# Retimed plan, squares of v as a step, half of the rest on POOL, weights two places on: attention, Fourier mixing and a feed-forward block on one core

## Chip, cores and metric

The kernel runs on one core of a Trainium2 chip. The metric is device time in microseconds (us), the median of several runs. Five engines of the core matter: PE (TensorE, matmuls; PEld is its weight load), DVE (VectorE), ACT (ScalarE), POOL (GpSimd) and SP (SyncE, which issues most DMAs). Each works through its own queue in order, and they wait for each other by semaphores. PSUM, where PE writes, has eight banks here: one for the value products, three called `ps`, two called `h` and two called `acc`.

## What is computed

Block-causal attention over 8 batches x 8 heads, 576 positions of 64 dimensions; then, for each batch, a two-dimensional Fourier transform whose real part is added to x, a normalization, and a feed-forward block 512 to 2048 to 512.

```python
scores = scale * np.matmul(q, k.transpose(0, 1, 3, 2))
scores = np.where(block_i >= block_j, scores, -1000000000.0)   # blocks of 64 positions
attn = np.exp(scores - np.max(scores, axis=-1, keepdims=True))
attn = attn / (np.sum(attn, axis=-1, keepdims=True) + 1e-09)
x = np.matmul(attn, v)                  # heads side by side: 8 x 576 x 512
u = x + np.real(np.fft.fft(np.fft.fft(x, axis=1), axis=2))
un = (u - np.mean(u, -1)) / np.sqrt(np.var(u, -1) + 1e-06)
out = u + np.maximum(un @ w_ch1, 0.0) @ w_ch2
```

## The kernel before

Numbers are carried as pairs: a high part that PE multiplies, and the rest that is left of it.

**Heads.** For each head, `load_head` brings q and k (`raw`), `lead` makes the rounded high part on ACT (L275), `lead_copies` sends two copies of it by SP's DMAs into the `rest` tile, and `rest` makes the two halves of the remainder, each 64 x 576, on DVE (L285, L286). `max_part` (four parts, n = 0 to 3) multiplies and reduces the row maxima on DVE (L358, and L361 for the last block); `shift` transposes them on PE (L183) and sends them as an additional row into `lead`. `scores` (four pieces) multiplies, takes the exponential twice on ACT (L401 in 16 bits, L402 in 32), and POOL subtracts (L403), so that `ph` and `pl` are the two parts of the probabilities. `values` multiplies them by v; at its end DVE computes `DEN`, its reciprocal and x (L438 to L441), which SP writes to `xd` for two heads at a time.

**v.** Once for two heads, `load_v` loads V (one buffer) and `split_v` makes it into `VH` and `VL`: ACT squares and sums V into `vacc` (two buffers; L299; its unused product goes into the scratch `tmp`), a matmul with ones sums over partitions, DVE makes a power of two from it (L304 to L308), ACT scales (L310) and DVE takes the remainder (L311). `DEN` reads the scale out of the same `vacc`.

**Fourier and feed-forward.** After a batch's eight heads, `mirror` reads `xd` back by POOL's indirect DMAs; `folded` adds on DVE (L517, L518, scratch `tmp`) and splits on ACT and DVE into `fs` (L485, L486); `stage1`, `stage2_sin` and `stage2_cos` multiply. `norm` and `turn` normalize and transpose. Each group of two tiles then gives one feed, whose steps `first` (tile `h`, then `gh` on ACT and `gl` on DVE) and `second` (tile `acc`) PE works through.

**Weights.** They come as 64-bit numbers. `weight_loads` lands them in parts of the big tile `W` that are still free, or in `stage`; `weight_single` turns them into 32 bits with six DVE instructions for two (L786, L788, L790), and ACT squares them (L792); `weight_scale` makes the scale; `weight_parts` writes the high part on ACT (L814) and the remainder on DVE (L815). The 32 bits of weight i lie in place i + 1 of `W`, which part i + 1 overwrites.

**The plan.** The order of work is made at build time by a planner. Each lane (heads, preparation, v, maxima, scores, values, transform) yields steps; a `Step` has its time on PE (`cost`), a `chain` of what follows on other engines, written as an engine letter with a duration ("A0.25", Q for SP's queue, L for latency, G for POOL), the steps it comes `after` in time, the steps that must only have been issued (`need`), and a `place` that sets who goes first. The planner keeps a booked queue for each engine, adds `HOP` between engines, and takes, of the steps that are ready, the one with the lowest place; if none is ready, PE gets a step of the current feed, the filler. A step that is ready only in less than `MARGIN` (0.3) waits while there is filler. PE keeps exactly this order. A step with `bank` takes a PSUM bank; until the first feeds, the banks of `h` and `acc` are lent as well. The order on the other engines is set when the program is built, out of the order in which steps were issued. The weights are a side lane, issued while the queue of the first engine of a step is short.

Of the kernel before, what the change touches and what calls it, by code (L numbers as in the profile page):

```python
# [20 lines left out]
DM = H * D  # L21
FF = 4 * DM
P = 128
# [9 lines left out]

HOP = 0.2
MARGIN = 0.3
# [7 lines left out]
KM = D + 8  # L43
KS = KM + 1


# [76 lines left out]
class Step:  # L123
# [12 lines left out]
    def __post_init__(self):  # L136
        self.chain = [(x[0], float(x[1:])) for x in self.chain]

# [26 lines left out]
def tile_attn_fourier_ffn(  # L165
# [61 lines left out]

    W = const.tile([P, 2 * NF + 1, 2, DM], F16, name="W")
    inv_w = const.tile([P, 1], F32, name="inv_w")
# [51 lines left out]

    def rest(h):

        x0, x1, raw = REST[h % NB], LEAD[h % NB].bitcast(F32), raws.pop(h)
        nc.vector.tensor_tensor(x0[0:D, 0:S], raw[:, 0:S], x1[0:D, 64:64 + S], op=ALU.subtract)  # L285
        nc.vector.tensor_tensor(x0[D:P, S:], raw[:, S:], x1[0:D, 64 + S:], op=ALU.subtract)  # L286

# [4 lines left out]
    vraw = {}  # L292

    def split_v(g):

        V = vraw.pop(g)
        acc = work.tile([P, 4], F32, name="vacc", bufs=2)
        junk = work.tile([P, DM], F32, name="tmp", bufs=2).bitcast(F16)[:, 0:5 * 2 * D]
        nc.scalar.activation(junk, V.rearrange("p c h d -> p (c h d)"), AF.Square, accum_out=acc[:, 0:1])  # L299
        t = ps_tile()  # L300
# [13 lines left out]
    def head_lane():  # L314
        for h in range(B * H):
            yield Step(
                lambda: load_head(h), 0.0, ("Q0.6", "L2.5"), (("T2", h - 2),) if h > 1 else (), ("L", h), place=h - 2.2
            )

    def prepare_lane():  # L320
        for h in range(B * H):
            yield Step(
                lambda: lead(h), 0.0, ("A1.05",), (("L", h),), ("T", h), place=h - 1.0,
                need=(("S", h - NB, 2),) if h >= NB else (),
            )
# [12 lines left out]

    def max_part(h, n):
# [9 lines left out]
        for i, (j, lo, hi) in enumerate(parts):  # L349
# [4 lines left out]
            at += hi - lo  # L354
        at = 0
        for j, lo, hi in parts:
            to = 5 if lo else j
            nc.vector.tensor_reduce(m[:, to:to + 1], t[:, at:at + hi - lo], axis=AX.X, op=ALU.max)  # L358
            at += hi - lo
        if n == 3:  # L360
            nc.vector.tensor_tensor(m[:, 4:5], m[:, 4:5], m[:, 5:6], op=ALU.max)  # L361

    MAXPARTS = (((0, 0, 64), (1, 0, 192), (4, 512, 576)), ((2, 0, 320),), ((3, 0, 448),), ((4, 0, 512),))

# [86 lines left out]
    def score_lane():  # L451
        for h in range(B * H):
            for n, (i, at, chunks) in enumerate(PIECES):
                w = sum(x[2] for x in chunks)
                e = 0.085 + 0.00083 * w
                yield Step(
                    lambda n=n: scores(h, n), w / 1200.0, (f"A{2 * e}", f"G{0.19 + 0.002 * w}"),
                    (("X", h), ("TC", h), ("T2", h)), ("S", h, i) if n else None, True,
                    need=(("V", h - 1, 2 * i),) if h else (), place=h,
                )  # L460

    def max_lane():
        for h in range(B * H):
            for n in range(4):
                yield Step(
                    lambda n=n: max_part(h, n), 0.05 + sum(x[2] - x[1] for x in MAXPARTS[n]) / 2000.0, (f"D{(0.6, 0.45, 0.55, 0.7)[n]}",),
                    (("T", h),), ("M", h) if n == 3 else None, True, place=h - 0.6,
                )
            yield Step(lambda: shift(h), 0.12, ("A0.25", "Q0.6", "L2.2"), (("M", h),), ("X", h), True, place=h - 0.6)

    def value_lane():
        for h in range(B * H):
            for n, c in enumerate(CHUNKS):
                yield Step(
                    lambda n=n: values(h, n), 0.09 * (5 - c), ("D0.9",) if n == 4 else (),
                    (("S", h, (0, 1, 1, 2, 2)[n]), ("N", h // 2)) + ((("V", h - 1, 4),) if h else ()), ("V", h, n),
# [13 lines left out]
    def fourier_steps(b):  # L490
# [125 lines left out]
        for name, op, width in (("c", ALU.add, 257), ("s", ALU.subtract, 256)):  # L616
            for c in (2, 0, 1):
                yield Step(
                    lambda c=c: folded(op, width, name, c), 0.0, ("D0.8", "A0.3", "D0.3"), (D_("u"),),
                    D_("f" + name) if c == 1 else None, place=place,  # L620
                )
            for m in range(2):
                yield Step(
                    lambda m=m: stage1(name, m), 0.87, ("A0.35", "D0.4"), (D_("f" + name),),
                    D_("z" + name) if m == 1 else None, True, place=place,
                )
            if name == "c":
                yield Step(stage1_tail, 0.62, ("A0.3", "D0.4"), (D_("fc"),), D_("zt"), True, place=place)
        for c in (2, 0, 1):
            yield Step(lambda: stage2_sin(c), 0.67, ("A0.3",), (D_("zs"),), D_("b", c), True, place=place)  # L630
            yield Step(
                lambda: stage2_cos(c), 0.78, ("D0.7", "D1.3" if b == 0 else "G2.4"), (D_("zc"), D_("zt"), D_("b", c)), D_("u", c), True,
                need=(("F", feed_number(b - 1, 2)),) if c == 2 and b == 4 else (), place=place,
            )
# [11 lines left out]
    def normalized_steps(us, keys, stores, place):  # L646
# [46 lines left out]
    def feed_steps(me, uh, ul, us, stores):  # L693
# [32 lines left out]
        def first_steps(f):  # L726
            for part in range(NK):
                last = part == NK - 1
                after = (("t", me, 0), ("t", me, 1)) + ((("g", me, f - 2),) if f > 1 else ()) if part == 0 else ()
                if me == 1:  # L730
                    after += (("w", NK * (f // NK) + part),)
                yield Step(
                    lambda part=part: first(f, part), 0.327, ("A0.3", "D0.35") if last else (), after,
                    ("g", me, f) if last else None,
                )

        def second_steps(f):
            for n in range(2):
                yield Step(
                    lambda n=n: second(f, n), 0.648, (), (("g", me, f),) + ((("w", NF + f),) if me == 1 else ()),  # L740
                    ("F", me) if f == NF - 1 and n == 1 else None,
# [20 lines left out]

    LANDS = [(17, 19, 21, 23)[i % 4] for i in range(NF)]
    LANDS += [25, 27, 29, 31, -1, -2, -3, 25, 27, 29, 31, -1, -2, -3, -1, -2]

# [15 lines left out]
    def weight_single(i):  # L781
        if loads[0] < i + 2:
            weight_loads(i)
        two = [(raw(j).rearrange("p (n x) -> p x n", x=2), W[:, j + 1].rearrange("p x n -> p (x n)").bitcast(I32)) for j in (i, i + 1)]
        for r, t in two:
# [24 lines left out]
    def weight_parts(i):  # L810
        t = W[:, i + 1].rearrange("p x n -> p (x n)").bitcast(F32)
        w = i // NF
        sc = wst[:, 4 * w + 1:4 * w + 2]
        nc.scalar.activation(W[:, i, 0], t, AF.Copy, scale=sc)  # L814
        nc.vector.scalar_tensor_tensor(W[:, i, 1], t, sc, W[:, i, 0], op0=ALU.mult, op1=ALU.subtract)  # L815

    def weight_lane():
        yield Step(lambda: weight_loads(0), 0.0, ("Q5",), (("L", 0),), ("load",))
        def single(i):
            return Step(  # L820
                lambda: weight_single(i), 0.0, ("D0.6", "D0.6", "D0.9", "D0.9", "D0.85", "D0.85", "A0.82", "A0.82"), (("load",),),
                "w32" if i == 2 * NF - 2 else None,
            )

        def scale(w):
            return Step(lambda: weight_scale(w), 0.1, ("D1.2",), (), ("scale", w), True)
# [128 lines left out]
```

## Time and profile before

| what | value |
|---|---|
| median of 3 runs | 1396.62 us (1396.25 to 1399.97) |
| profiled execution | 1401.47 us, its span 1399.7 us |
| mean granted TensorE clock | 0.938 |
| instructions | 25596 |
| memory traffic | 58.46 MB read, 18.87 MB written |

The profile lists busy times by engine, the same in slices or windows of time, groups of instructions by line, and waits. Most matmuls stand at one helper's line, L180, and transpositions at L183, so they are told apart by their tiles: `ps<-vacc,ones` is the sum over partitions of `split_v`, `ps<-ident,M` the transposition of `shift`. A row of waits names the engine that waited, its line and tile, what released it, the total, how often and the longest. A group's row gives count, busy time and mean ns of one instruction, then idle time just before it and who ended it. A timeline row gives start and duration in us, then in brackets the idle time before and its releaser.

### The profile page before, as it was taken

Reading aid. Unit: us, or ns where it says so; the run is one execution under the profiler, and the core shown is the slowest. Engines: PE = TensorE matmul, PEld = TensorE weight load, DVE = VectorE, ACT = ScalarE, POOL = GpSimd, SP = SyncE. Lnnn points to the kernel's source line nnn. Section 1 sums busy time; section 2 is a strip of 40 time slices with the busy share of each in tenths; the row PEclk is TensorE's granted clock in tenths of the full one; section 3 lists DMA queues with packets and bytes.
Section 4 is the critical chain, followed back from the end, with each engine's and each line's share of the span. In section 5 each row is a group of like instructions: output and inputs, shape, how many; then the busy total and the mean of one; then the engine's idle time right before and its main releaser. Section 6 shows DMA issues by size and latency. Waiting matters only on the chain.

```text
span 1399.7 us, 25596 instructions
## 1 busy us (share of the span) xinstructions
PE 1203.7 (86%) x10068; PEld 895.2 (64%) x10068; DVE 748.2 (53%) x1770; ACT 568.0 (41%) x1293; POOL 383.5 (27%) x484
## 2 busy tenths in 40 slices
PE   2546478988897999889998999898989899999998
PEld 1445356766675677566675767676667676766665
DVE  5996776456645564555537555755464634322211
ACT  3555546444453445443444444444443342111111
POOL 1323122232423243324232522343232431300000
PEclk9965679999899999989999999999999999999999
DMA  9655212232223112421322122312222101000000
GB/s 289 192 174 177 62 29 77 70 95 57 59 63 108 49 43 69 111 57 28 93 73 73 32 67 73 107 32 68 62 92 57 42 10 58 5 16 16 16 16 15
DMA packets 56168, 99.11 MB, mean 71 GB/s; under 512 B 7933, under 2 KB 26829, under 8 KB 55920
## 3 DMA queue, kind: packets, MB, share of 16 engines
q1 hardware_dynamic: 53760, 89.94, 23.0%
q0 software_dynamic: 2288, 7.54, 1.7%
q8 instruction: 79, 1.29, 0.4%
q14 instruction: 41, 0.34, 0.1%
HBM read 58.46 MB, written 18.87 MB: 55 GB/s over the span
## 4 chain that ended last, share of the span: by engine, by line
PE 66%; DVE 16%; DMA 7%; issue 4%; POOL 3%; ACT 3%; SPq 0%; DVEq 0%; POOLq 0%; ACTq 0%
PE acc L180 24%; PE h L180 24%; PE ps L180 14%; PE av L180 3%; DVE rest L286 2%; DVE rest L285 2%; DVE M L358 2%; DMA U<-xd,rows 2%; PE ps L183 2%; DMA V<-in_v_dram 1%; DVE W L790 1%; DVE W L788 1%; DMA W<-in_moe_w_ch_dram 1%; ACT tmp L299 1%; DVE tmp L517 1%
## 5 line engine op out<-in xcount | busy, mean ns | idle before, releaser
L180 PE MATMUL h<-uh,W 128*128 128x256 f16 x2304 | 455.4, 278 | 0.0
L403 POOL TENSOR_TENSOR pl<-p,ph 128x288 f16<-128x288 f32 (+1 forms) x256 | 245.5, 969 | 572.0 <-ACT p L402 477.6
L180 PEld LDWEIGHTS <-W 128*128 128x128 f16 x3456 | 330.9, 100 | 88.6 <-issue 4.2
L180 PE MATMUL acc<-W,gh 128*128 128x512 f16 x1152 | 352.1, 388 | 0.6 <-ACT gh L711 0.6
L180 PE MATMUL h<-ul,W 128*128 128x256 f16 x1152 | 319.3, 277 | 0.7 <-DVE ul L674 0.7
L712 DVE SCALAR_TENSOR_TENSOR gl<-h,gh 128x256 f16<-128x256 f32 x288 | 121.6, 422 | 358.1 <-ACT gh L711 356.0
L711 ACT ACTIVATE gh<-h 128x256 f16<-128x256 f32 x288 | 110.8, 385 | 360.4 <-PE h L180 351.9
L180 PE MATMUL acc<-W,gl 128*128 128x512 f16 x576 | 222.4, 386 | 3.7 <-DVE gl L712 3.7
L180 PE MATMUL ps<-lead 72*128 72x64 f32 (+2 forms) x714 | 210.5, 353 | 7.0 <-DVE vacc L304 3.6
L358 DVE TENSOR_REDUCE M<-ps 128x1 f32<-128x192 f32 (+2 forms) x353 | 138.3, 427 | 96.4 <-PE ps L180 95.6
L401 ACT ACTIVATE ph<-ps 128x512 f16<-128x512 f32 (+1 forms) x238 | 122.0, 513 | 86.0 <-PE ps L180 83.4
L180 PEld LDWEIGHTS ps<-lead 72*128 72x128 f32 (+1 forms) x714 | 131.7, 204 | 21.1 <-DVE vacc L304 4.2
L180 PEld LDWEIGHTS <-gh 128*128 128x128 f16 x1152 | 102.7, 100 | 59.6 <-issue 3.9
L180 PE MATMUL av<-VH,ph 128*128 128x65 f16 x960 | 122.0, 205 | 18.4 <-DVE x L441 17.5
L180 PEld LDWEIGHTS <-ph 128*128 128x128 f16 x1920 | 107.6, 104 | 47.3 <-issue 23.4
L180 PE MATMUL av<-VH,pl 128*128 128x65 f16 x960 | 118.7, 202 | 19.8 <-POOL pl L403 19.7
L402 ACT ACTIVATE p<-ps 128x512 f32<-128x512 f32 (+1 forms) x238 | 122.4, 514 | 18.0 <-POOL pl L403 17.8
L180 PE MATMUL ps<-rest 128*128 128x192 f32 (+4 forms) x361 | 123.1, 349 | 0.5 <-ACT p L402 0.5
L180 PE MATMUL av<-VL,ph 128*128 128x64 f16 x960 | 120.3, 202 | 0.0
L180 PEld LDWEIGHTS <-pl 128*128 128x128 f16 x960 | 95.1, 103 | 23.7 <-POOL pl L403 23.4
L180 PEld LDWEIGHTS <-gl 128*128 128x128 f16 x576 | 57.3, 99 | 76.3 <-DVE gl L712 5.9
L180 PEld LDWEIGHTS ps<-rest 128*128 128x128 f32 x361 | 72.4, 201 | 10.5 <-ACT p L402 0.7
(171 smaller groups left out, 1310.3 us busy)
## 6 DMA issues: line engine op xcount, KB each, us to landing
raw<-in_qk_dram SPq DMA_DIRECT2D x64, 288.0 KB
rest<-lead SPq DMA_DIRECT2D x128, 144.0 KB
W<-in_moe_w_ch_dram SPq DMA_DIRECT2D x24, 512.0 KB
V<-in_v_dram SPq DMA_DIRECT2D x32, 320.0 KB
xd<-x SPq DMA_DIRECT2D x32, 256.0 KB
out_dram<-u SPq DMA_DIRECT2D x32, 256.0 KB
u<-in_moe_w_ch_dram SPq DMA_DIRECT2D x8, 512.0 KB
u<-xd SPq DMA_DIRECT2D x8, 512.0 KB
```

What stands on the lines that cost most here:

```text
L180: return tc.keep_in_program_order(nc.tensor.matmul(*args, **kw))
L183: return tc.keep_in_program_order(nc.tensor.transpose(*args, **kw))
L285: nc.vector.tensor_tensor(x0[0:D, 0:S], raw[:, 0:S], x1[0:D, 64:64 + S], op=ALU.subtract)
L286: nc.vector.tensor_tensor(x0[D:P, S:], raw[:, S:], x1[0:D, 64 + S:], op=ALU.subtract)
L299: nc.scalar.activation(junk, V.rearrange("p c h d -> p (c h d)"), AF.Square, accum_out=acc[:, 0:1])
L358: nc.vector.tensor_reduce(m[:, to:to + 1], t[:, at:at + hi - lo], axis=AX.X, op=ALU.max)
L401: nc.scalar.activation(ph[:, at:at + w], t[:, 0:w], AF.Exp, scale=0.125)
L402: nc.scalar.activation(p32[:, 0:w], t[:, 0:w], AF.Exp, scale=0.125)
L403: nc.gpsimd.tensor_tensor(pl[:, at:at + w], p32[:, 0:w], ph[:, at:at + w], op=ALU.subtract)
L517: nc.vector.tensor_tensor(e[0:r], X[c][0:r], U[c][0:r], op=op)
L711: nc.scalar.activation(gh, t, AF.Relu)
L712: nc.vector.scalar_tensor_tensor(gl, t, 0.0, gh, op0=ALU.max, op1=ALU.subtract)
```

## The change

It has seven parts.

1. The durations in the chains are replaced by others, also for the steps of Fourier and normalization, and `HOP` goes from 0.2 to 0.25. Formulas for a width are given to ACT, DVE and POOL.
2. A chain may hold a "B": the PSUM bank counts as free from there, not from the chain's end.
3. The square and sum of V leave `split_v` and become a step of their own, `sum_v`, with the same `need`; `split_v` comes after it.
4. `rest` is two steps: the first half stays on DVE, the second goes to POOL. `load_head` and `scores` come after both.
5. In the first part of the maxima, one reduction with two results replaces two, and the order of the blocks changes.
6. `weight_parts` of the first matrix (i below 16) scales a second time on ACT, into the scratch `un`, and POOL subtracts; the second matrix's stays.
7. The 32 bits of weight i lie in place i + 2 of `W`, which has one place more, and the landing places move by one.

```diff
-HOP = 0.2
+HOP = 0.25
...
+def _a(width):
+    return f"A{0.19 + 0.00082 * width}"
...
+def _d(width):
+    return f"D{0.19 + 0.00102 * width}"
...
+def _g(width):
+    return f"G{0.19 + 0.00194 * width}"
...
+        free = None
         for engine, cost in step.chain:
-            t = t + cost if engine == "L" else queues[engine].book(t + HOP, cost)
+            if engine == "B":
+                free = t + HOP
+            else:
+                t = t + cost if engine == "L" else queues[engine].book(t + HOP, cost)
...
-            rings[current] = rings[current][1:] + [t]
+            rings[current] = rings[current][1:] + [t if free is None else free]
...
-        nc.vector.tensor_tensor(x0[D:P, S:], raw[:, S:], x1[0:D, 64 + S:], op=ALU.subtract)
+            nc.gpsimd.tensor_tensor(x0[D:P, S:], raw[:, S:], x1[0:D, 64 + S:], op=ALU.subtract)
...
+    def sum_v(g):
+        acc = vsums[g] = work.tile([P, 4], F32, name="vacc", bufs=2)
+        junk = work.tile([P, DM], F32, name="tmp", bufs=2).bitcast(F16)[:, 0:5 * 2 * D]
+        nc.scalar.activation(junk, vraw[g].rearrange("p c h d -> p (c h d)"), AF.Square, accum_out=acc[:, 0:1])
...
-            yield Step(lambda: rest(h), 0.0, ("D0.65", "D0.65"), (("T", h),), ("T2", h), place=h - 0.8)
+            yield Step(lambda: rest(h, 0), 0.0, (_d(S),), (("T", h),), ("T2", h, 0), place=h - 0.8)
+            yield Step(lambda: rest(h, 1), 0.0, (_g(S),), (("T", h),), ("T2", h, 1), place=h - 0.8)
...
+            yield Step(lambda: sum_v(g), 0.0, ("A0.95",), (("LV", g),), ("NS", g), place=2 * g - 0.6,
+                       need=(("V", 2 * g - 3, 4),) if g > 1 else ())
             yield Step(
-                lambda: split_v(g), 0.1, ("D0.3", "A0.8", "D0.8"), (("LV", g),), ("N", g), True,
+                lambda: split_v(g), 0.11, ("D0.46", "B", "A0.83", "D0.88"), (("NS", g),), ("N", g), True,
                 need=(("V", 2 * g - 3, 4),) if g > 1 else (), place=2 * g - 0.4,
...
+        if n == 0:
+            nc.vector.tensor_reduce(
+                m[:, 0:6:5], t[:, 0:128].rearrange("p (x y) -> p x y", y=64), axis=AX.X, op=ALU.max
+            )
+        j, lo, hi = parts[-1]
+        nc.vector.tensor_reduce(m[:, j:j + 1], t[:, at - hi:at], axis=AX.X, op=ALU.max)
...
-                    lambda n=n: scores(h, n), w / 1200.0, (f"A{2 * e}", f"G{0.19 + 0.002 * w}"),
+                    lambda n=n: scores(h, n), w / 1200.0, (_a(w), _a(w), "B", _g(w)),
...
-                    lambda n=n: max_part(h, n), 0.05 + sum(x[2] - x[1] for x in MAXPARTS[n]) / 2000.0, (f"D{(0.6, 0.45, 0.55, 0.7)[n]}",),
+                    lambda n=n: max_part(h, n), 0.03 + sum(x[2] - x[1] for x in MAXPARTS[n]) / 2400.0, (f"D{(0.65, 0.49, 0.63, 0.93)[n]}",),
...
-            yield Step(lambda: shift(h), 0.12, ("A0.25", "Q0.6", "L2.2"), (("M", h),), ("X", h), True, place=h - 0.6)
+            yield Step(lambda: shift(h), 0.12, ("A0.26", "B", "Q0.6", "L2.2"), (("M", h),), ("X", h), True, place=h - 0.6)
...
-                    lambda c=c: folded(op, width, name, c), 0.0, ("D0.8", "A0.3", "D0.3"), (D_("u"),),
+                    lambda c=c: folded(op, width, name, c), 0.0, ("D1.6", "A1.2", "D0.9") if c == 2 else ("D1.12", "A0.41", "D0.43"), (D_("u"),),
...
-    W = const.tile([P, 2 * NF + 1, 2, DM], F16, name="W")
+    W = const.tile([P, 2 * NF + 2, 2, DM], F16, name="W")
...
     def weight_parts(i):
-        t = W[:, i + 1].rearrange("p x n -> p (x n)").bitcast(F32)
+        t = W[:, i + 2].rearrange("p x n -> p (x n)").bitcast(F32)
         w = i // NF
         sc = wst[:, 4 * w + 1:4 * w + 2]
         nc.scalar.activation(W[:, i, 0], t, AF.Copy, scale=sc)
+        if w == 0:
+            scaled = work.tile([P, DM], F32, name="un", bufs=2)
+            nc.scalar.activation(scaled, t, AF.Copy, scale=sc)
+            nc.gpsimd.tensor_tensor(W[:, i, 1], scaled, W[:, i, 0], op=ALU.subtract)
+            return
         nc.vector.scalar_tensor_tensor(W[:, i, 1], t, sc, W[:, i, 0], op0=ALU.mult, op1=ALU.subtract)
...
-            return Step(lambda: weight_parts(i), 0.0, ("A0.72", "D0.7"), (("scale", i // NF),), ("w", i))
+            return Step(lambda: weight_parts(i), 0.0, ("A1.45", "G1.2") if i < NF else ("A0.73", "D0.75"), (("scale", i // NF),), ("w", i))
```

More of the change, by code (lines that the diff above doesn't have):

```diff
@@ L136, in __post_init__ @@
     def __post_init__(self):
-        self.chain = [(x[0], float(x[1:])) for x in self.chain]
+        self.chain = [(x[0], float(x[1:] or 0.0)) for x in self.chain]
 class Queue:
@@ L280, in lead_copies, with rest @@
         nc.sync.dma_start(x0[0:D, S:], x1[0:D, 64 + S:])
[L282 to L286, printed above, removed]
+    def rest(h, which):
+        x0, x1, raw = REST[h % NB], LEAD[h % NB].bitcast(F32), raws[h]
+        if which == 0:
+            nc.vector.tensor_tensor(x0[0:D, 0:S], raw[:, 0:S], x1[0:D, 64:64 + S], op=ALU.subtract)
+        else:
+            nc.gpsimd.tensor_tensor(x0[D:P, S:], raw[:, S:], x1[0:D, 64 + S:], op=ALU.subtract)
     def load_v(g):
@@ L292, in tile_attn_fourier_ffn @@
     vraw = {}
+    vsums = {}
+    def sum_v(g):
+        acc = vsums[g] = work.tile([P, 4], F32, name="vacc", bufs=2)
+        junk = work.tile([P, DM], F32, name="tmp", bufs=2).bitcast(F16)[:, 0:5 * 2 * D]
+        nc.scalar.activation(junk, vraw[g].rearrange("p c h d -> p (c h d)"), AF.Square, accum_out=acc[:, 0:1])
     def split_v(g):
+        acc = vsums.pop(g)
         V = vraw.pop(g)
-        acc = work.tile([P, 4], F32, name="vacc", bufs=2)
-        junk = work.tile([P, DM], F32, name="tmp", bufs=2).bitcast(F16)[:, 0:5 * 2 * D]
-        nc.scalar.activation(junk, V.rearrange("p c h d -> p (c h d)"), AF.Square, accum_out=acc[:, 0:1])
         t = ps_tile()
@@ L316, in head_lane @@
             yield Step(
[L317 removed]
+                lambda: load_head(h), 0.0, ("Q0.6", "L2.5"), (("T2", h - 2, 0), ("T2", h - 2, 1)) if h > 1 else (), ("L", h), place=h - 2.2
             )
@@ L322, in prepare_lane @@
             yield Step(
-                lambda: lead(h), 0.0, ("A1.05",), (("L", h),), ("T", h), place=h - 1.0,
+                lambda: lead(h), 0.0, ("A1.15",), (("L", h),), ("T", h), place=h - 1.0,
                 need=(("S", h - NB, 2),) if h >= NB else (),
@@ L354, in max_part @@
             at += hi - lo
[L355 to L359, printed above, removed]
+        if n == 0:
[4 more added lines that the diff above has]
+        nc.vector.tensor_reduce(m[:, j:j + 1], t[:, at - hi:at], axis=AX.X, op=ALU.max)
         if n == 3:
             nc.vector.tensor_tensor(m[:, 4:5], m[:, 4:5], m[:, 5:6], op=ALU.max)
-    MAXPARTS = (((0, 0, 64), (1, 0, 192), (4, 512, 576)), ((2, 0, 320),), ((3, 0, 448),), ((4, 0, 512),))
+    MAXPARTS = (((0, 0, 64), (4, 512, 576), (1, 0, 192)), ((2, 0, 320),), ((3, 0, 448),), ((4, 0, 512),))
     def shift(h):
@@ L732, in first_steps @@
                 yield Step(
-                    lambda part=part: first(f, part), 0.327, ("A0.3", "D0.35") if last else (), after,
+                    lambda part=part: first(f, part), 0.327, ("A0.4", "D0.44") if last else (), after,
                     ("g", me, f) if last else None,
@@ L760, in weight @@
         return w2[P * (i - NF):P * (i - NF + 1)]
-    LANDS = [(17, 19, 21, 23)[i % 4] for i in range(NF)]
-    LANDS += [25, 27, 29, 31, -1, -2, -3, 25, 27, 29, 31, -1, -2, -3, -1, -2]
+    LANDS = [(18, 20, 22, 24)[i % 4] for i in range(NF)]
+    LANDS += [26, 28, 30, 32, -1, -2, -3, 26, 28, 30, 32, -1, -2, -3, -1, -2]
     def raw(i):
@@ L783, in weight_single @@
             weight_loads(i)
-        two = [(raw(j).rearrange("p (n x) -> p x n", x=2), W[:, j + 1].rearrange("p x n -> p (x n)").bitcast(I32)) for j in (i, i + 1)]
+        two = [(raw(j).rearrange("p (n x) -> p x n", x=2), W[:, j + 2].rearrange("p x n -> p (x n)").bitcast(I32)) for j in (i, i + 1)]
         for r, t in two:
```

23 lines of the change are left out of this document (11 added, 12 removed).

## The prediction

> **What bounds the kernel now.** First the page's busy times, then the same by stage (the view of windows: busy time and instruction count of each engine, granted clock, DMA share, GB/s).
>
> ```profile
> PE 1203.7 (86%) x10068; PEld 895.2 (64%) x10068; DVE 748.2 (53%) x1770; ACT 568.0 (41%) x1293; POOL 383.5 (27%) x484
> ...
> 0.00:210.00 210.00, 109.03 (x778) 89.41 (x779) 162.94 (x357) 105.83 (x233) 52.20 (x65) 0.76 0.52 154
> ...
> 245.00:1155.00 910.00, 826.09 (x7341) 619.88 (x7339) 494.17 (x1208) 397.85 (x908) 304.95 (x382) 0.96 0.24 65
> ...
> 1190.00:1400.00 210.00, 205.51 (x1422) 140.48 (x1419) 52.35 (x117) 34.14 (x88) 12.32 (x22) 1.00 0.04 14
> ```
>
> There are three stages with three limits. From 0 to 210 us PE is busy 109 us and DVE 163 us: weights are decoded on DVE, and PE waits. From 245 to 1155 us PE is busy 826 of 910 us, so 84 us are lost. From 1190 us on only the feed-forward steps remain, and PE is full. This last stage matters: the planner fills PE with feed-forward steps whenever attention isn't ready, and 210 us of them are still left at the end. So filler never runs out in the middle stage, and a microsecond of waiting saved there is a microsecond saved at the end. Who ends the 84 us is in the waits of PE in that window (line waited for, us in total, times, longest):
>
> ```profile
> PE ps L180 <- ACT tmp L299: 34.8, 12, 6.4
> PE ps L183 <- DVE M L361: 19.3, 15, 3.7
> PE av L180 <- POOL pl L403: 16.0, 20, 2.6
> PE ps L183 <- DVE DEN L438: 7.3, 8, 0.9
> ...
> PE ps L180 <- ACT p L402: 1.0, 2, 0.5
> ```
>
> The first row is the sum of v's squares: PE stands at the matmul over partitions until ACT has squared V. The second and fourth are one thing, the transposition of the row maxima in `shift`, 26.6 us in 23 waits. The third is the low half of the probabilities, which POOL makes. Together they are 77 of the 84 us. One wait of the first kind, and the engines behind another:
>
> ```profile
> 450.84 0.20 PE L180 MATMUL av<-VH,pl 128*128 128x65 f16 x1
> 455.87 0.59 PE L180 MATMUL ps<-vacc,ones 128*128 128x1 f32 x2 [4.84 <-ACT tmp L299]
> ```
> ```profile
> 693.48 0.21 DVE L438 TENSOR_SCALAR DEN<-av,vacc 128x5 f32<-128x5 f32 x1
> ...
> 693.73 0.74 ACT L299 ACTIVATE tmp<-V 128x640 f16<-128x640 f32 x1 [2.08 <-DVE DEN L438]
> 694.37 0.19 ACT L299 ACTIVATION_READ_ACCUMULATOR tmp<-V 128x1 f32 x1
> ```
> ```profile
> 454.99 0.74 ACT L299 ACTIVATE tmp<-V 128x640 f16<-128x640 f32 x1 [0.99 <-DVE fs L486]
> ```
>
> The matmul stands right behind the last value product of a head. At 693 us ACT waits for DVE's DEN, the last reader of the accumulator's buffer (there are two), and then squares for 0.83 us. In the long wait, at 455 us, it waited for a Fourier step's `fs` besides: the square's scratch, `tmp`, is shared with that step. The planner's entry for this step has no time ahead of its matmul, so nothing was put between.
>
> **The change part by part.** The sum is made against the profiled execution, 1401.5 us (its span of 1399.7 and 1.8 around it), 4.9 us above the median of 1396.6; the difference is carried to the median unchanged.
>
> *Squares as a step.* `sum_v` is issued under the same condition as before (the head two places back is through), and `split_v` only when the plan says that the squares are there: two hops of 0.25 and 0.95 us, 1.45 us, and 0.3 us of margin when filler is at hand. So about 1.6 us of other PE work comes between. Of the 12 waits, three are long, about 5.4 us each (one of 4.84 is shown, the row's longest is 6.4), and keep the rest: 3 x 1.6 = 4.8 us. The other nine hold 34.8 - 16.2 = 18.6 us, 2.07 each; I take 1.6 off each, 14.4 us. Bounds: nothing, if ACT gets the square later by as much; 34.8 us, if all goes. **Sum: -19 us.** No new DMA and no wait on SP goes with it. Behind the waiting square on ACT stand exponentials as before.
>
> *Durations.* The rows that the plan now carries, and those of the halves that move:
>
> ```profile
> L358 DVE TENSOR_REDUCE M<-ps 128x1 f32<-128x512 f32 x57 | 39.3, 689 | 25.1 <-PE ps L180 24.5
> L361 DVE TENSOR_TENSOR M<-M 128x1 f32<-128x1 f32 x64 | 13.2, 207 | 0.9
> L358 DVE TENSOR_REDUCE M<-ps 128x1 f32<-128x64 f32 x118 | 25.4, 215 | 13.3 <-PE ps L180 13.3
> L285 DVE TENSOR_TENSOR rest<-raw,lead 64x576 fp32r<-64x576 f32 x64 | 52.2, 816 | 16.8 <-ACT lead L275 16.7
> L286 DVE TENSOR_TENSOR rest<-raw,lead 64x576 fp32r<-64x576 f32 x64 | 49.0, 765 | 0.9
> L403 POOL TENSOR_TENSOR pl<-p,ph 128x512 f16<-128x512 f32 x128 | 151.1, 1184 | 71.8 <-ACT p L402 66.9 <-PE h L180 2.7 <-PE ps L180 1.9
> L403 POOL TENSOR_TENSOR pl<-p,ph 128x288 f16<-128x288 f32 x128 | 94.6, 754 | 500.2 <-ACT p L402 410.7 <-PE ps L180 88.5
> ```
>
> The last part of the maxima takes 689 + 207 = 0.90 us; the plan said 0.7 and now says 0.93, with 0.1 us more for hops. So `shift` comes about 0.3 us later. Against 26.6 us in 23 waits, 1.16 each, that is 23 x 0.3 = 7 us. Now a typical one:
>
> ```profile
> 418.68 0.69 DVE L358 TENSOR_REDUCE M<-ps 128x1 f32<-128x512 f32 x1 [0.72 <-PE ps L180]
> 419.29 0.74 DVE L285 TENSOR_TENSOR rest<-raw,lead 64x576 fp32r<-64x576 f32 x1
> 420.04 0.75 DVE L286 TENSOR_TENSOR rest<-raw,lead 64x576 fp32r<-64x576 f32 x1
> 420.82 0.16 DVE L361 TENSOR_TENSOR M<-M 128x1 f32<-128x1 f32 x1
> ```
> ```profile
> 421.13 0.27 PE L183 MATMUL ps<-ident,M 128*5 128x128 f32 x1 [0.91 <-DVE DEN L438]
> ```
>
> Both halves of the next head's rest slipped in ahead of the maximum. Without the second, M would be ready 0.75 us earlier, if POOL leaves DVE alone (below). I take 3 us more, four such waits: **-10 us** for `shift`; bounds 0 and -26.6. The merged reduction of 128 elements lies on the line between the rows of 64 and 512, 215 + 64 x 1.06 = 0.28 us, in place of 2 x 0.215: 64 x 0.15 = 10 us of DVE, hidden under PE. The bank that is free at "B" lets the plan issue scores about 1.2 us (the 512-wide POOL row) earlier; with filler at hand this only changes the order: nothing. If the bank isn't free, PE would wait on ACT p, now 1.0 us in all.
>
> *Rest on POOL.* From the two L403 rows: (1184 - 754)/224 = 1.92 ns an element, so 576 take 1.31 us; bounds 1.18 (the 512 row) and 1.6. Times 64 this is 84 us more on POOL, 27% to 33% of the span; 49 us leave DVE. Behind it on POOL stand the subtractions that the value products wait for, and on SP the next raw load, which needs both halves but has two heads of time. The price is in whether both engines run at once:
>
> ```profile
> 309.30 2.26 POOL L403 TENSOR_TENSOR pl<-p,ph 128x512 f16<-128x512 f32 x2
> ```
> ```profile
> 309.83 2.28 DVE L517 TENSOR_TENSOR tmp<-X,U 33x512 f32<-33x512 f32 x1 [0.27 <-DMA U<-xd,rows]
> ```
> ```profile
> L517 DVE TENSOR_TENSOR tmp<-u 128x512 f32<-128x512 f32 x32 | 21.8, 683 | 0.2
> L517 DVE TENSOR_TENSOR tmp<-X,U 33x512 f32<-33x512 f32 x16 | 18.2, 1140 | 28.4 <-DMA U<-xd,rows 28.4
> ```
>
> They don't: a DVE subtraction of two SBUF tensors that takes 0.68 us took 2.28 and ended 0.55 us after POOL's pair. DVE's remaining half and POOL's new half start from the same signal, so one waits for the other: DVE 0.74 us if it is first, 1.31 + 0.74 = 2.05 if POOL is; the mean, 1.40, is near the 1.58 of the two rows now. So this part is **0 us** on DVE, and +3 us for longer waits on POOL's pl: bounds -5 and +20.
>
> The Trainium skill, GPSIMD Engine Reference, section "8. Key points", says that POOL shares its SBUF interfaces with VectorE and contends with DVE instructions that have two SBUF inputs; the pair at 309 us agrees. Its section "4.1 Engine selection" would keep such work on VectorE, about 2 times faster; the rows give 1.31 to 0.75 us. By that rule the part is a loss; its case is the rival on the slow side.
>
> *Weights.*
>
> ```profile
> L814 ACT ACTIVATE W<-W,wst 128x512 f16<-128x512 f32 x32 | 23.1, 722 | 17.5 <-DVE W L815 17.3
> L815 DVE SCALAR_TENSOR_TENSOR W<-W,wst 128x512 f16<-128x512 f32 x32 | 23.9, 747 | 9.7 <-ACT W L814 9.6
> ```
> ```profile
> 139.00:172.00 33.00, 11.71 (x16) 0.58 0.22 63
> ```
> ```profile
> 139.00:172.00 33.00, 14.48 (x78) 10.66 (x76) 24.94 (x49) 18.00 (x35) 5.32 (x7) 0.58 0.22 63
> ```
>
> ACT and DVE take turns (17.3 and 9.6 us of waiting on each other), since a part overwrites what the one before still reads. Two places further on, they overlap. The first 16 parts lie from 139 to 172 us (the first of the two windows rows is of L815 alone, 16 instructions on DVE; the second is of all), beside the first Fourier step, where PE is busy 14.5 of 33 us and DVE 24.9. There DVE loses 16 x 0.747 = 12 us, ACT gains 16 x 0.722 = 11.6, POOL 16 x 1.18 = 19. Fully on the path, -12; if POOL blocks DVE's Fourier subtractions each time, +7. I take **-7 us**, nearer the first, as DVE has idle time to give there too.
>
> *Clock.* In the middle stage it stands at 0.96, so 0.04 x 910 = 36 us of clock were withheld, around the long stalls. I give back a third, the share of the 84 us of waits that goes (30 of 84): **-12 us**; bounds 0 and -36.
>
> The Trainium skill, TensorE: Matmul & The Clock Gate, section "Part 1: The HAM clock gate", has the clock fall to half after an idle window of about 3.4 us; no view here shows the window itself, and a clock of 0.96 beside waits of up to 6.4 us agrees with it. By that rule waits of 2 us would cost no clock, and the term would shrink to the three long ones, some -6.
>
> Sum: -19 - 10 + 3 - 7 - 12 = -45: 1401.5 becomes 1356.5, and the median 1396.6 becomes **1352 us**.
>
> **The rivals.**
> *The waits move* (1384 us). The square is still released by the same DEN, and the plan doesn't know of scratch buffers or of engines that block each other. The middle stage gains 19 + 10 - 3 + 12 = 38 us above; if two thirds of it come back as waits on POOL or the scratch, and the start gains nothing, 1396.6 - 13 = 1384. For it: the wait of 4.84 us was such a buffer. Against: 1.6 us of filler behind each head is certain once the plan holds the step back. The case in which the step is issued as early as before, and so does nothing, is its upper end, 1397.
> *POOL and DVE block each other* (1419 us). Each of the 56 heads past the start has a POOL half of 1.31 us in front of its pl and before DVE's half. If most of that, 1.2 us, reaches PE in each, that is 56 x 1.2 = +67, against -45: 1396.6 + 22 = 1419. It decides from 45/56 = 0.8 us a head. For it: the pair at 309 us. Against: rest is made a whole head before its scores, and POOL idles two thirds of the span.
> *All waits go* (1302 us). The rows of `sum_v`, `shift` and pl end (77 us) and half the withheld clock comes back (18), with a start as now: 1396.6 - 95 = 1302. For it: the plan now carries the durations of these very rows. Against: it knows neither the scratch buffers nor the blocking.
>
> **How the numbers follow.** Forecast 0.50 (1330 to 1370), all waits go 0.16, the waits move 0.20 (of which 0.07 within 0.3%), blocking 0.14. A measurement of this kernel tells about 0.3%, 4.2 us, from no change. So faster 0.79, same 0.07, slower 0.14. The range reaches from 1310, in the rival of all waits, to 1393, the end of the moved waits; outside are blocking and the lowest 0.05.
>
> **What would show it.** PE's waits on ACT tmp in the middle stage should fall from 34.8 to about 16 us, those of `shift` from 26.6 to 17, PE's busy share rise, the clock reach 0.97. DVE's rest and Fourier subtractions longer than 1 us, and more than 16 us on POOL pl, would speak for blocking. The alternation L814/L815 should be gone, and PE be busy for more than 109 of the first 210 us. I am wrong if it isn't, or if a new row of PE waits above 15 us stands in the middle.

## The result and the profile after

The changed kernel takes 1332.5 us (median of 4 runs, 1329.4 to 1335.2) beside 1396.4 us of the kernel before: a ratio of 0.9536, 95% interval 0.9507 to 0.9565. That is 64 us less, where 45 were forecast. The profiled execution has a span of 1328.7 us, 71 us below the 1399.7 of before, whose profiled execution, at 1401.5 us, lay above its four timed runs.

The page's busy times of the changed kernel, then its view of windows, cut where the rows of before were cut (stretch, PE, PEld, DVE, ACT, POOL, granted clock, DMA share, GB/s):

```profile
PE 1190.9 (90%) x10068; PEld 890.2 (67%) x10068; DVE 701.5 (53%) x1626; ACT 573.0 (43%) x1309; POOL 526.6 (40%) x564
```
```profile
0.00:210.00 210.00, 112.15 (x827) 93.18 (x828) 151.16 (x329) 121.49 (x261) 106.98 (x96) 0.79 0.53 157
...
245.00:1155.00 910.00, 875.50 (x7733) 656.11 (x7732) 489.10 (x1158) 403.32 (x934) 402.28 (x450) 0.99 0.25 67
```

PE's idle time fell from 1399.7 - 1203.7 = 196.0 us to 1328.7 - 1190.9 = 137.8, so by 58 us; PE's busy time fell by 13 us for the same 10068 matmuls. The two make the 71 us. Most of the first, 49 us, is the middle stage: from 245 to 1155 us the loss went from 84 to 34.5 us. The second goes with the clock, 0.96 to 0.99 in that stage. The first 210 us hold 3 us more of PE's work. POOL is busy 143 us longer, DVE 47 us shorter.

PE's waits in the middle stage of the changed kernel (what waited for what, total, times, longest):

```profile
PE av L192 <- POOL pl L430: 8.5, 7, 3.4
PE ps L195 <- DVE M L388: 7.6, 5, 3.4
PE ps L192 <- DVE M L386: 7.2, 5, 2.7
...
PE ps L192 <- ACT p L429: 1.3, 1, 1.3
PE ps L195 <- ACT p L429: 1.3, 1, 1.3
...
PE ps L192 <- ACT tmp L317: 0.7, 1, 0.7
```

The row for ACT tmp has 0.7 us left of 34.8. The transposition of the maxima (now L195) waits 7.6 us for them and 1.3 for ACT, in place of 26.6. New is PE's waiting for the maxima at L192, 7.2 us, which was 0.7; no new row comes near the 15 us that the prediction named as a sign of being wrong. Even POOL's pl, for which the prediction added 3 us, costs half of the 16.0 it did.

The first norm, the end of the first Fourier step, comes at 168.3 us in place of 175.8 (the fields behind the median are the first and the last start; before, then after):

```profile
L657 DVE BATCH_NORM_STATS2 st<-u x32: 664/685/696, 175.8 to 1216.8; 128x6 f32<-128x512 f32 x32
```
```profile
L683 DVE BATCH_NORM_STATS2 st<-u x32: 665/678/695, 168.3 to 1132.9; 128x6 f32<-128x512 f32 x32
```

The turns that ACT and DVE took at the weights, 17.3 and 9.6 us of waiting for each other before, are gone, as the prediction asked (1.6 and 1.8 us):

```profile
L840 ACT ACTIVATE W<-W,wst 128x512 f16<-128x512 f32 x32 | 22.5, 719 | 3.5 <-DVE wst L831 1.7 <-DVE W L846 1.6
...
L846 DVE SCALAR_TENSOR_TENSOR W<-W,wst 128x512 f16<-128x512 f32 x16 | 13.7, 877 | 1.9 <-ACT W L840 1.8
```

One more view tells something that the prediction had not looked at: the instructions of the line that makes x, one for each head, with the start of the first and of the last. First the kernel before, then the changed one:

```profile
L441 DVE TENSOR_TENSOR x<-av,rec x64: 469/491/492, 47.9 to 1153.5; 128x320 f32<-128x320 f32 x64
```
```profile
L468 DVE TENSOR_TENSOR x<-av,rec x64: 459/491/492, 47.6 to 956.3; 128x320 f32<-128x320 f32 x64
```

The last head is done at 956 us in place of 1154, although the whole is only 64 us shorter: the feed-forward steps, which PE took in between, now stand at the end. A batch of heads follows the one before every 117 us in place of 145 ((956.3 - 139.6)/7 and (1153.5 - 141.9)/7, by the starts of the eighth and the last head's x).

### The profile page after: what moved, and what is told of

Its sections match the earlier page's. It is cut to its first block, busy times and chain, and to the rows that moved or that the text cites. A ratio compares the mean times of both kernels' runs of the same rounds, so it can differ in the third digit from the quotient of the medians.

```text
span 1328.7 us, 25730 instructions
## 1 busy us (share of the span) xinstructions
PE 1190.9 (90%) x10068; PEld 890.2 (67%) x10068; DVE 701.5 (53%) x1626; ACT 573.0 (43%) x1309; POOL 526.6 (40%) x564
## 4 chain that ended last, share of the span: by engine, by line
PE 71%; DVE 13%; DMA 4%; ACT 4%; POOL 3%; issue 3%; SPq 0%; DVEq 0%; POOLq 0%; ACTq 0%
PE acc L192 25%; PE h L192 24%; PE ps L192 15%; PE av L192 5%; DVE M L386 2%; DVE tmp L543 1%; DMA W<-in_moe_w_ch_dram 1%; PE ps L195 1%; DMA U<-xd,rows 1%; DVE W L814 1%; DVE W L812 1%; DVE W L816 1%; POOL pl L430 1%; POOL u L532 1%; DVE rest L302 1%
## 5 line engine op out<-in xcount | busy, mean ns | idle before, releaser
L192 PE MATMUL h<-uh,W 128*128 128x256 f16 x2304 | 450.8, 275 | 0.0
L430 POOL TENSOR_TENSOR pl<-p,ph 128x288 f16<-128x288 f32 (+1 forms) x256 | 258.5, 1019 | 355.2 <-issue 170.5
L192 PEld LDWEIGHTS <-W 128*128 128x128 f16 x3456 | 324.9, 99 | 88.2 <-issue 5.3
L192 PE MATMUL acc<-W,gh 128*128 128x512 f16 x1152 | 347.4, 383 | 0.0
L192 PE MATMUL h<-ul,W 128*128 128x256 f16 x1152 | 315.7, 274 | 0.1
L192 PE MATMUL acc<-W,gl 128*128 128x512 f16 x576 | 220.0, 382 | 1.9 <-DVE gl L738 1.8
L192 PE MATMUL ps<-lead 72*128 72x320 f32 (+5 forms) x711 | 205.1, 347 | 18.5 <-DMA lead<-mt 10.1
L192 PEld LDWEIGHTS ps<-lead 72*128 72x128 f32 (+1 forms) x711 | 129.5, 202 | 27.5 <-DMA lead<-mt 10.4
L192 PEld LDWEIGHTS <-gh 128*128 128x128 f16 x1152 | 100.3, 100 | 64.7 <-issue 6.8
L386 DVE TENSOR_REDUCE M<-ps 128x1 f32<-128x320 f32 (+2 forms) x239 | 123.5, 528 | 37.7 <-PE ps L192 36.5
L192 PEld LDWEIGHTS <-ph 128*128 128x128 f16 x1920 | 113.8, 104 | 41.0 <-DVE x L468 18.9
L192 PE MATMUL av<-VH,ph 128*128 128x65 f16 x960 | 119.0, 203 | 20.2 <-DVE x L468 8.9
L192 PE MATMUL av<-VH,pl 128*128 128x65 f16 x960 | 117.3, 201 | 19.1 <-POOL pl L430 19.0
L192 PE MATMUL ps<-rest 128*128 128x288 f32 (+1 forms) x354 | 125.1, 360 | 2.8 <-ACT p L429 1.3
L192 PE MATMUL av<-VL,ph 128*128 128x64 f16 x960 | 118.2, 200 | 0.0
L304 POOL TENSOR_TENSOR rest<-raw,lead 64x576 fp32r<-64x576 f32 x64 | 111.2, 1738 | 17.7 <-ACT lead L291 13.4
L192 PEld LDWEIGHTS <-pl 128*128 128x128 f16 x960 | 94.4, 103 | 21.8 <-POOL pl L430 21.3
L192 PEld LDWEIGHTS <-gl 128*128 128x128 f16 x576 | 56.6, 98 | 74.0 <-DVE gl L738 5.5
```

The source lines that it names most:

```text
L192: return tc.keep_in_program_order(nc.tensor.matmul(*args, **kw))
L304: nc.gpsimd.tensor_tensor(x0[D:P, S:], raw[:, S:], x1[0:D, 64 + S:], op=ALU.subtract)
L386: nc.vector.tensor_reduce(m[:, j:j + 1], t[:, at - hi:at], axis=AX.X, op=ALU.max)
L430: nc.gpsimd.tensor_tensor(pl[:, at:at + w], p32[:, 0:w], ph[:, at:at + w], op=ALU.subtract)
```

## The experiments

All were timed against the kernel before, which had medians of 1395.2 to 1398.0 us in these sets. Where a kernel is compared with one of another set, the difference is that of their ratios to before, times 1396 us. Gains over the kernel before are differences of medians; by the ratios they come out 1 to 2 us smaller.

### The squares' step alone, and taken away

The kernel before with part 3 alone:

```diff
+            yield Step(lambda: sum_v(g), 0.0, ("A0.95",), (("LV", g),), ("NS", g), place=2 * g - 0.6,
+                       need=(("V", 2 * g - 3, 4),) if g > 1 else ())
...
-                lambda: split_v(g), 0.1, ("D0.3", "A0.8", "D0.8"), (("LV", g),), ("N", g), True,
+                lambda: split_v(g), 0.1, ("D0.3", "A0.8", "D0.8"), (("NS", g),), ("N", g), True,
```

> The kernel before with part 3 alone: squares as their own step, the old durations. Predicted sizes: 19 us of waits and 6 to 10 of clock less, 1368 to 1372. If the step only helps with true durations in the plan, 1385 to 1397.

1367.3 us, ratio 0.9795 (0.9758 to 0.9832): 31 us less than its 1398.0. PE's waits in the middle stage, longest rows:

```profile
PE ps L183 <- DVE M L368: 25.4, 19, 4.4
PE av L180 <- POOL pl L410: 9.4, 17, 1.5
PE ps L183 <- DVE DEN L445: 7.9, 9, 1.3
PE ps L180 <- ACT tmp L299: 6.1, 1, 6.1
```

The wait for the squares fell from 34.8 to a single one of 6.1 us: 29 us of it go, where 19 were expected. But the waits for the maxima grew, from 26.6 to 33.3 us (25.4 + 7.9). The whole stage:

```profile
245.00:1155.00 910.00, 844.32 (x7532) 631.95 (x7530) 509.29 (x1239) 403.22 (x924) 307.77 (x387) 0.98 0.24 67
```

PE loses 66 of the 910 us in place of 84, so 18 less, close to the 19. The rest of the 31 us comes mostly with shorter matmuls: PE is busy 1191.9 us in place of 1203.7.

The other way round, the changed kernel with the squares back inside `split_v`:

```diff
+        sum_v(g)
         acc = vsums.pop(g)
...
-            yield Step(lambda: sum_v(g), 0.0, ("A0.95",), (("LV", g),), ("NS", g), place=2 * g - 0.6,
-                       need=(("V", 2 * g - 3, 4),) if g > 1 else ())
...
-                lambda: split_v(g), 0.11, ("D0.46", "B", "A0.83", "D0.88"), (("NS", g),), ("N", g), True,
+                lambda: split_v(g), 0.11, ("D0.46", "B", "A0.83", "D0.88"), (("LV", g),), ("N", g), True,
```

> The changed kernel with part 3 undone: the squares of v are made inside split_v again, all else as changed. If the squares' step is the largest term, as predicted (19 us of waits and part of the 12 of clock), the time lies 25 to 35 us above the changed kernel, 1358 to 1367, and PE waits for ACT tmp some 30 us in the middle stage. If the retimed plan does the work and the step only adds to it, PE meets ACT later anyway and the time is within 10 us of 1332.

1356.1 us, ratio 0.9693 (0.9647 to 0.9740), 22 us above the changed kernel. Its waits for ACT tmp in the middle stage:

```profile
PE ps L192 <- ACT tmp L317: 15.9, 18, 1.7
```

They are 15.9 us, not 30, and none is longer than 1.7 us. So something else in the change had already halved these waits and removed the long ones.

### The plan: durations and bank marks

The kernel before with parts 1 and 2 alone (all new durations, HOP, and the marks "B"):

```diff
-HOP = 0.2
+HOP = 0.25
...
-                    lambda n=n: scores(h, n), w / 1200.0, (f"A{2 * e}", f"G{0.19 + 0.002 * w}"),
+                    lambda n=n: scores(h, n), w / 1200.0, (_a(w), _a(w), "B", _g(w)),
```

> The kernel before with parts 1 and 2 alone: new durations, HOP and the early release of banks, no other change. Predicted sizes: 10 us off shift and 3 to 4 of clock, 1380 to 1386. If the plan's durations are the main cause, 1350 to 1370, and the waits for M and for pl fall by half or more while those for ACT tmp stay at 35.

1353.6 us, ratio 0.9693 (0.9658 to 0.9728): 44 us less, far beyond the 10 to 16 of the sizes as predicted. But the waits for ACT tmp didn't stay at 35 us, as was expected even if the durations were the main cause:

```profile
PE ps L192 <- ACT tmp L317: 10.4, 9, 2.3
PE ps L195 <- DVE M L386: 8.4, 9, 2.0
PE acc L192 <- DVE gl L736: 8.4, 7, 3.7
```

So the two halves of it were tried apart. First the durations without the marks:

```diff
-                    lambda n=n: scores(h, n), w / 1200.0, (_a(w), _a(w), "B", _g(w)),
+                    lambda n=n: scores(h, n), w / 1200.0, (_a(w), _a(w), _g(w)),
```

> The kernel before with the new durations and HOP, but without the marks B: a bank counts as held to the end of a chain. The durations with B gave 1353.6. If the durations alone do it, 1348 to 1360 and the batches follow each other every 115 to 120 us as with B. If the early release of banks is what quickens attention, 1375 to 1395 and a batch takes some 140 us or more, since the longer chains now hold the banks longer in the plan.

1388.7 us, ratio 0.9954 (0.9934 to 0.9973): 7 us less than before, and no more. Then the marks without the durations (all but the one of `weight_scale`):

```diff
-                    lambda n=n: scores(h, n), w / 1200.0, (f"A{2 * e}", f"G{0.19 + 0.002 * w}"),
+                    lambda n=n: scores(h, n), w / 1200.0, (f"A{2 * e}", "B", f"G{0.19 + 0.002 * w}"),
...
-            yield Step(lambda: shift(h), 0.12, ("A0.25", "Q0.6", "L2.2"), (("M", h),), ("X", h), True, place=h - 0.6)
+            yield Step(lambda: shift(h), 0.12, ("A0.25", "B", "Q0.6", "L2.2"), (("M", h),), ("X", h), True, place=h - 0.6)
```

> The kernel before with the marks B alone, old durations and HOP. The prediction priced this at nothing: 1390 to 1400. If the release is the larger part of what the durations with B gave, 1355 to 1375, batches every 115 to 125 us and the waits for ACT tmp well below 34.8 us, since other steps then stand between.

1384.1 us, ratio 0.9926 (0.9910 to 0.9943): 12 us less. Alone they give 7 and 12 us, together 44: most of it comes only when both are there. The squares' waits, with the durations alone and with the marks alone:

```profile
PE ps L192 <- ACT tmp L317: 38.2, 13, 8.7
```
```profile
PE ps L180 <- ACT tmp L303: 30.5, 15, 2.9
```

With both they were 10.4. The order on PE tells a part of it: of the 32 matmuls that sum the squares over partitions, 22 stand directly behind a value product in the kernel before, with no other work between; 15 with the durations alone, 11 with the marks alone, 6 with both. It isn't the whole: with the marks alone 8 of the 15 waits, 14.5 of the 30.5 us, come behind other work. The last head's x tells another part, with the durations alone, the marks alone, and both:

```profile
L466 DVE TENSOR_TENSOR x<-av,rec x64: 474/491/493, 46.6 to 1171.6; 128x320 f32<-128x320 f32 x64
```
```profile
L445 DVE TENSOR_TENSOR x<-av,rec x64: 473/491/492, 54.4 to 907.6; 128x320 f32<-128x320 f32 x64
```
```profile
L466 DVE TENSOR_TENSOR x<-av,rec x64: 471/491/492, 47.2 to 954.9; 128x320 f32<-128x320 f32 x64
```

The marks quicken attention: 908 and 955 us with them, 1172 and 1154 without. (The squares' step alone quickens it too, though less: 1096 us.) In the plan of before, a bank of the three `ps` was held to the end of the step's chain. After `scores` that is the end of POOL's subtraction, about 1.2 us after the last reader for 512 columns; after `shift` it is the landing of its DMA, 0.6 + 2.2 us later by the plan's own entries; after `split_v` it is ACT's and DVE's work, 0.8 + 0.8 us. With no bank free in the plan, PE gets filler instead of the next attention step. The marks were only tried together, so which of them counts is open. The windows from 245 to 960 and on to 1155 us show what pace is worth, in PE's busy time; first the kernel before, then the marks alone, then both:

```profile
245.00:960.00 715.00, 643.82 (x5686) 483.70 (x5684) 393.18 (x963) 313.81 (x713) 239.91 (x304) 0.96 0.25 68
960.00:1155.00 195.00, 182.28 (x1657) 136.18 (x1656) 100.99 (x246) 84.04 (x195) 65.04 (x78) 0.97 0.19 53
```
```profile
245.00:960.00 715.00, 646.45 (x6055) 491.43 (x6055) 437.79 (x1048) 350.97 (x803) 279.11 (x326) 0.97 0.28 77
960.00:1155.00 195.00, 192.19 (x1336) 133.79 (x1335) 74.94 (x169) 41.50 (x107) 36.24 (x58) 1.00 0.08 26
```
```profile
245.00:960.00 715.00, 668.20 (x6311) 512.43 (x6309) 450.36 (x1078) 365.03 (x830) 286.86 (x333) 0.98 0.29 79
960.00:1155.00 195.00, 193.16 (x1339) 134.65 (x1338) 77.56 (x176) 41.23 (x106) 43.31 (x69) 1.00 0.07 23
```

While heads run, PE loses about a tenth (71 of 715 us before, 69 with the marks alone). Once they are through, almost nothing: from 960 to 1155 us it loses 13 us of 195 before, where heads still run, and 3 and 2 with the marks, where they don't. The marks shorten the stretch in which PE can lose; with the true durations besides, the loss in it falls to 47 us and the clock rises. That the same steps lose less because others stand between is argued from the counts above, not shown: which step stands where was not tried singly. Why the two together give so much more than 7 and 12 us stays open.

The changed kernel without the five marks shows that this still holds with the squares' step there. One of them:

```diff
-            yield Step(lambda: shift(h), 0.12, ("A0.26", "B", "Q0.6", "L2.2"), (("M", h),), ("X", h), True, place=h - 0.6)
+            yield Step(lambda: shift(h), 0.12, ("A0.26", "Q0.6", "L2.2"), (("M", h),), ("X", h), True, place=h - 0.6)
```

> The changed kernel without the marks B, all else as changed. If the early release is as much part of the gain as the two small runs say (B on top of the durations gave 35 us), the time is 1355 to 1375 and a batch takes 135 us or more again. If it only mattered while the squares had no step of their own, 1332 to 1342.

1371.0 us, ratio 0.9813 (0.9784 to 0.9842), 39 us above the changed kernel, and attention ends at 1155.7 us again. Of the 32 sums of squares 15 stand directly behind a value product, beside 7 in the changed kernel. Kernels whose order differs for other reasons (the runs below that alter hops, rest or weights singly) lie within 5 us of the changed one, so 39 us isn't chance of the order. Of its profiled 44.6 us more, 26 are idle time of PE and 18 longer matmuls (1373.3 - 1209.1 = 164.2 us idle beside 137.8):

```profile
PE 1209.1 (88%) x10068; PEld 900.5 (66%) x10068; DVE 708.8 (52%) x1626; ACT 575.8 (42%) x1309; POOL 525.1 (38%) x564
```

Is it only slack that the plan lacked? The changed kernel with a longer hop:

```diff
-HOP = 0.25
+HOP = 0.4
```

> The changed kernel with HOP at 0.4 in place of 0.25, so that each handover is planned later than the trace shows it. If it is the slack in the plan that ends PE's waits, the 34 us that PE still loses in the middle stage fall to 20 or less and the time is 1312 to 1325. If true durations and free banks are what counts, nothing is left to win by slack: 1330 to 1345.

1333.8 us, ratio 0.9551 (0.9524 to 0.9579): no difference from the changed kernel, and PE loses 35 us in the middle stage, as there. More slack wins nothing.

### Rest on POOL

Both halves of rest back on DVE:

```diff
-            nc.gpsimd.tensor_tensor(x0[D:P, S:], raw[:, S:], x1[0:D, 64 + S:], op=ALU.subtract)
+            nc.vector.tensor_tensor(x0[D:P, S:], raw[:, S:], x1[0:D, 64 + S:], op=ALU.subtract)
...
-            yield Step(lambda: rest(h, 1), 0.0, (_g(S),), (("T", h),), ("T2", h, 1), place=h - 0.8)
+            yield Step(lambda: rest(h, 1), 0.0, (_d(S),), (("T", h),), ("T2", h, 1), place=h - 0.8)
```

> The changed kernel with both halves of rest on DVE. If POOL and DVE exclude each other, as the prediction held, the move is worth about nothing: 1325 to 1338, and POOL loses the 111 us of L304, pl gets faster. If the move is what relieved DVE ahead of the maxima, the time rises by 10 us or more (1342 and up) and PE waits longer for M.

1333.9 us, ratio 0.9557 (0.9522 to 0.9592): the same as the changed kernel. The move is worth nothing that these runs can tell. Two heads of the changed kernel show why; the half on DVE, then the half on POOL:

```profile
428.57 0.94 DVE L302 TENSOR_TENSOR rest<-raw,lead 64x576 fp32r<-64x576 f32 x1 [0.99 <-ACT lead L291]
...
441.63 1.50 DVE L302 TENSOR_TENSOR rest<-raw,lead 64x576 fp32r<-64x576 f32 x1
```
```profile
428.97 1.81 POOL L304 TENSOR_TENSOR rest<-raw,lead 64x576 fp32r<-64x576 f32 x1
441.10 1.41 POOL L304 TENSOR_TENSOR rest<-raw,lead 64x576 fp32r<-64x576 f32 x1
```

At 428 us DVE comes first and POOL's half takes 1.81 us; at 441 us POOL is first with 1.41 us, and DVE's half takes 1.50 in place of 0.74. The groups have both cases mixed:

```profile
L304 POOL TENSOR_TENSOR rest<-raw,lead 64x576 fp32r<-64x576 f32 x64 | 111.2, 1738 | 17.7 <-ACT lead L291 13.4
...
L302 DVE TENSOR_TENSOR rest<-raw,lead 64x576 fp32r<-64x576 f32 x64 | 62.3, 973 | 83.0 <-ACT lead L291 71.6 <-PE av L192 11.0 <-DMA xd<-x 0.4
```

DVE gives up 49.0 us of the second half and pays 10 us more on the first (62.3 beside 52.2); POOL pays 111 us, 27 more than was worked out.

With rest on DVE throughout, the first norm had come at 162.4 us in place of 168.3, so rest was put on DVE for the first ten heads and on POOL after them:

```diff
+            engine = nc.vector if h < 10 else nc.gpsimd
+            engine.tensor_tensor(x0[D:P, S:], raw[:, S:], x1[0:D, 64 + S:], op=ALU.subtract)
...
```

> The changed kernel with the second half of rest on DVE for the first ten heads and on POOL after them. With all of rest on DVE the first norm came at 162.4 us in place of 168.3, and the middle stage lost 3 us. If the two sum up, 1325 to 1330, faster than the changed kernel. If the earlier norm was chance of the order, 1330 to 1338.

1333.1 us, ratio 0.9543 (0.9518 to 0.9569): the same again. The earlier norm didn't hold (165.6 us in this one) and gave nothing at the end.

### Weights

The remainders of the first matrix back on DVE, with one scaling on ACT:

```diff
-        if w == 0:
-            scaled = work.tile([P, DM], F32, name="un", bufs=2)
-            nc.scalar.activation(scaled, t, AF.Copy, scale=sc)
-            nc.gpsimd.tensor_tensor(W[:, i, 1], scaled, W[:, i, 0], op=ALU.subtract)
-            return
...
```

> The changed kernel with part 6 undone: all remainders of the weights on DVE, one scaling on ACT. If the 12 us of DVE that part 6 takes away lie on the path of the first Fourier step, the first norm comes 5 to 10 us later than 168.3 us and the time is 1337 to 1342. If POOL's 16 subtractions block DVE as much as they relieve it, 1328 to 1336.

1335.9 us, ratio 0.9572 (0.9557 to 0.9588), first norm at 167.8 us beside 168.3: not told apart from the changed kernel. And the weights one place on, with PE's order unchanged:

```diff
-        t = W[:, i + 2].rearrange("p x n -> p (x n)").bitcast(F32)
+        t = W[:, i + 1].rearrange("p x n -> p (x n)").bitcast(F32)
...
```

> The changed kernel with the weights one place on, as before (part 7 undone); the order on PE is the same instruction for instruction. If the turns of ACT and DVE lay on the path, the first norm comes 3 to 7 us later than 168.3 and the time is 1335 to 1340. If the first 16 parts, bound by two scalings each on ACT, hide it, 1330 to 1335.

1335.8 us, ratio 0.9562 (0.9538 to 0.9586), first norm at 169.2: not told apart either, although ACT and DVE wait for each other again (6.8 and 6.4 us). Parts 1 to 3 without any of the others, so that the changed kernel loses parts 4 to 7; besides the two edits above and that of rest:

```diff
-        if n == 0:
-            nc.vector.tensor_reduce(
-                m[:, 0:6:5], t[:, 0:128].rearrange("p (x y) -> p x y", y=64), axis=AX.X, op=ALU.max
-            )
...
```

> The kernel before with parts 1, 2 and 3 alone: plan and squares' step, while rest, maxima and weights stay as they were. If the plan and the step are the whole gain of the middle stage and the rest is worth 5 to 10 us at the start, 1335 to 1343. If POOL's work and the weights carry no gain at all, 1329 to 1335; if they carry more than predicted, 1345 and up.

1340.8 us, ratio 0.9604 (0.958 to 0.9629). This interval lies above that of the changed kernel, so parts 4 to 7 together are worth 9 us or so (0.9604 - 0.9536 is 0.7% of 1396), though none of those that were undone singly (4, 6 and 7) shows by itself. The first norm comes at 173.1 us in this one and at 168.3 in the changed kernel, which is 5 of the 9 us. It is also the kernel with parts 1 and 2 and the squares' step added: 12 us less than without it (0.9693 to 0.9604). Part 5, the merged maximum, was not tried alone.

No version that was run beats the changed kernel.

## Why the prediction was right, and where not

**What bounds the kernel** held: PE with filler always at hand, so that waits removed in the middle stage come off the end. The 84 us fell to 34.5, and the span by 71.

**Squares as a step, -19 us**: the mechanism was right. Alone it took 29 us off the waits for the squares, 18 off all that PE loses in the middle stage, and 31 us of time, some 12 of them in shorter matmuls. Added to parts 1 and 2 it gives 12 us, taken out of the changed kernel it costs 22, so the parts' gains overlap. The prediction took the plan's 1.6 us off most waits; in fact all but one of the twelve ended. What PE does in each gap was not followed.

**Durations, -10 us**: near what they are by themselves, 7 us. The waits for the maxima, which the term was made from, fell from 26.6 to 11.9 us with them:

```profile
PE ps L195 <- DVE M L386: 11.9, 7, 7.4
```

**The bank marks, nothing**: this is the step that failed. "With filler at hand this only changes the order" took the order to be free. The marks alone gave 12 us, on top of the durations 36 (0.9954 to 0.9693), and without them the changed kernel is 39 us slower. They were the largest of the terms that were undone singly, and what hid it in the argument was that the middle stage was taken as a fixed length of time. It is not: its end is where attention ends, and PE loses most while attention runs. Also, the prediction weighed the bank of `scores` alone (1.2 us); `shift` held its bank longer.

**Rest on POOL, 0 us on DVE and +3 for pl**: that the move gains no time is confirmed, to within the measurement, but not the sum behind it. POOL and DVE take turns in the trace, as it was read from the one pair at 309 us; yet DVE's half was worked out at 1.40 us and takes 0.97 on average, since it is held up to 1.5 us or more in 10 of 64 heads only, not in half. So DVE did gain 39 us (49.0 - 10), and they are worth nothing measurable. The second had the wrong sign: waits for pl fell from 16.0 to 8.5 us. They were 8.4 with both halves on DVE, and 16.7 with rest on POOL and all the weights' remainders on DVE: they follow the order of the instructions more than POOL's load.

**Weights, -7 us**: the first norm moved from 175.8 to 168.3 us, 7.5 earlier, but neither part 6 nor part 7 taken back moves it by more than 1 us. The turns of ACT and DVE did end, and having them back in part costs nothing measurable. Near the changed kernel, both parts are missing together only in the one with parts 1 to 3 (173.1 us), which lacks 4 and 5 as well; so one of the two may do the other's work, or another part is the cause. The number was met, its reason is not shown.

**Clock, -12 us**: PE's busy time fell by 13 us for the same matmuls, in one profiled execution each. That the two agree is in part luck: the kernels that take the same time as the changed one (rest, weights, hops) have 1193.7 to 1199.8 us beside its 1190.9 and the 1203.7 of before. So the term is some 4 to 13 us, and the -6 that the prediction gave as the other reading isn't ruled out.

**The rivals**: moved waits and the slow side are out. POOL and DVE do hold each other up, as in the slow one, but these engines have time to spare. Of the 77 us that would have gone if all waits went, 59 did (0.7 + 7.6 + 1.3 + 8.5 = 18 are left), so the result lies between the forecast and that rival. The sum was 45 and the result 64, since one term counted at nothing was worth 36 to 39 us. The result lies 2.5 us inside the lower end of the forecast's range; that the range held with such a term left out is in part luck.

## What to carry to other kernels

A plan that holds a buffer longer than its last reader does slows down the work that needs the buffer, and filler hides it: PE looks busy, the order looks harmless, and the loss shows as waits elsewhere. That is what the marks showed here, though not which of them. So ask of every stage not only how much it loses but what sets its length. Terms that are put down at nothing because other work fills the gap should be tried by themselves, in both directions, since here two of 7 and 12 us made 44 together.

## What the runs showed of the hardware

POOL's subtraction of 64x576 takes about 1.40 us when DVE's half is not running as it starts (18 of the 64) and about 1.80 when it starts beside a running one (29); 17 lie outside these two groups. DVE's takes 0.72 to 0.94 us in 51 heads, and 1.5 to 2.0 in the ten in which POOL's was already running. The two pairs shown take 2.21 and 2.03 us from the first start to the last end, about the sum of both alone (1.40 + 0.74 = 2.14): running them side by side wins next to nothing. For POOL even the undisturbed 1.40 us is more than the 1.31 that its other subtractions led to expect; those write 16 bits, this one 32, and whether that is the reason was not tried.

Idle time of PE and slower matmuls came together: without the marks, 26 us more of idle time came with 18 us of slower matmuls, and a clock of 0.96 in place of 0.99 in the middle stage. Part of the 18 can be the spread between executions, which is up to 9 us among kernels of the same time (1190.9 to 1199.8).
